# Mixer output weights moved into the value region of the ring, multiplied on four column groups and summed by an fp32 matmul

## The chip, the cores and the metric

The kernel runs on one core of one Trainium2 chip. The metric is the device time of one execution in microseconds (us). The time before is the median of nine runs; the profile is that of one execution. Engines: PE (matmul), DVE (vector), ACT (scalar), POOL (general), SP (here it only issues DMAs).

## What is computed

One decode step of a gated mix of two branches, all tensors in bf16, one token, width 1024:

```python
g = sigmoid((x * gate_w).sum(-1))
# branch a: 32 query heads, 4 key/value heads, 65536 cached positions, head size 128
q = x @ wq                                   # wq 1024 x 4096
a = softmax(q k^T / sqrt(128)) v  @ wo       # k, v: 4 x 65536 x 128 each; wo 4096 x 1024
# branch b: gated MLP over one position
z = gelu(x @ w_in)                           # w_in 1024 x 3584
z1, z2 = halves of z;  z2 = layernorm(z2)
b = (z1 * (w_sp * z2 + b_sp)) @ w_out        # w_out 1792 x 1024
out = g * a + (1 - g) * b
```

The two caches are 64 MiB each. All that is loaded comes to 162 MB.

## The kernel before

**Ordering.** Every instruction is recorded with the keys that it reads and writes (`Recorder.op`), and `plan` turns these into semaphore waits. Each engine runs its own instructions in the order in which they were recorded. A load waits until the last readers and writers of its slots are done, and SP issues the loads strictly in the order of the list `stream`: a load that waits holds up all behind it.

**The ring.** All large loads go into one ring of five areas of 4 MiB (32 KB on each partition). The first three are taken in turn by `kring()`; the last two together are the value region `VB`, which holds 8 MiB. `issue()` (L360) puts a load into SP's program as soon as the kernel's text has marked the earlier contents of its slots as used (`done`). The order of the loads is: the query weights (VB, two DMAs), K pages 0 and 1, the mixer's input weights `w_in` (VB, two DMAs), K pages 2 and 3, the mixer's output weights `w_out` (next ring slot, 3.5 MiB), and then six times a K page, a value load of two pages (VB, two DMAs) and a K page; at the end the last values and `wo`. A K page has 4 MiB; there are 16, four for each key/value head. L373 is the line of all these loads, on SP's queue.

**Start.** Small tables are built from an identity matrix (L389 to L406). x and the gate weights are loaded by ACT's queue (L279, called at L286 and L287) as two rows of 512. x is turned into columns by a product with two rows of the identity (L409) and eight matmuls (L414). The gate takes a product, a sum and a small matmul (L424 to L431). Then come the query matmuls on four column groups of PE (recorded at L442), and the query tables.

**K steps.** `k_step(n)` handles a K page in four pieces: DVE transposes a piece (L483, two buffers `ktb`), PE multiplies it with the padded queries (L493; all matmuls of the helper `mm` show L253 or L255). `score_piece` (L500) moves the scores to SBUF and takes their maximum. For pages that begin a head, `q_piece` (L471) first writes that head's queries. `exp_piece` (L516, ACT), `pt_piece` (L521, DVE) and `pv_piece` (L531, PE, into `obt`) handle the values of earlier pages inside later steps.

**Mixer.** `mixer_piece` (after K page 1) multiplies x with `w_in` into `obt`, and DVE and ACT do gelu and the normalisation (L595 to L625) up to `yb`, the 1792 inputs of the last product as 14 columns. `wout_piece` (after K page 3) multiplies them with `w_out` in 14 x 2 matmuls (L635), all into one partition of `obt`, and four ACT copies (L641) spread this row over partitions 0, 32, 64 and 96 of `brow`.

**End.** The `wo` matmuls (L706) run on four column groups and add up in `fbt`; DVE adds `brow` (L712), and SP writes the result (L715).

The order of the steps in the program, before:

```python
k_step(1, evac=0, own=True)
mixer_piece()
k_step(2)
k_step(3, evac=2)
wout_piece()
```

Of the kernel before, what the change touches and what calls it, by code (L numbers as in the profile page):

```python
# [8 lines left out]
ACTF = mybir.ActivationFunctionType  # L9
ALU = mybir.AluOpType  # L10
AXX = mybir.AxisListType.X
# [127 lines left out]
def bass_gated_mix__gqa_block_cached__mixer_gmlp__decode_kernel(  # L139
# [23 lines left out]
    FC = FH // 128  # L163
    OC = HQ * Dh // 128
# [10 lines left out]
    QW = DO // 4  # L175
# [15 lines left out]
    for name, n in [  # L191
        ("RING", NSUB * SUB), ("KT", NKT * 4096), ("SC", NSC * 2048), ("PSB", 1024), ("PTSB", 2 * 1024),
        ("QPAD", 4 * QP), ("IDB", 128), ("BM", 256), ("SEL", 16 * 32),
        ("M16", 32), ("MQ", 32), ("XT", KC), ("WB", 2), ("WBB", 4), ("ONEB", 128),
        ("MAXC", 2 * total), ("LP", 2 * total), ("COLS", 2 * 64), ("DM", 32), ("QALL", 128), ("OV", OC), ("MHALF", 4),
        ("YB", FC), ("BROW", 2 * QW), ("OROW", QW),
    ]:
        region(name, n)
    NA = (cur + 63) // 64 * 64
# [2 lines left out]
    def ab(name, n, o=0):  # L202
        return arena[:, OFF[name] + o:OFF[name] + o + n]

    def af(name, n, o=0):
        return arena[:, OFF[name] + 2 * o:OFF[name] + 2 * (o + n)].bitcast(F32)

    def vw(base, off, dims, p0=0, np_=128):
        ps = base.ap[0][0]
        return bass.AP(tensor=base.tensor, offset=base.offset + off + p0 * ps,  # L210
                       ap=[[ps, np_]] + [list(d) for d in dims])

    idb, bm, ones = ab("IDB", 128), af("BM", 128), af("SC", 128, 4 * 1024 + 896)
    sel, m16, mq = ab("SEL", 512), af("M16", 16), af("MQ", 16)
    xT, wb, wbb, oneb = ab("XT", KC), ab("WB", 2), af("WBB", 2), ab("ONEB", 128)
    qpad, qall = ab("QPAD", 4 * QP), ab("QALL", 128)
    maxc, lp, colt = af("MAXC", total), af("LP", total), af("COLS", 64)
    mhalf = af("MHALF", 2)
    yb, ovec, orow, brow = ab("YB", FC), ab("OV", OC), ab("OROW", QW), af("BROW", QW)
    dm = af("DM", 16)  # L220
    psb = ab("PSB", 1024)
    osc, ot = ab("PSB", 512), af("PSB", 128, 256)
    col = lambda i: colt[:, i:i + 1]
    (C_GS, C_GE, C_G1, C_G, C_OMG, C_MU, C_V, C_S0, C_R0, C_S1, C_R1, C_AL, C_BE, C_T) = range(14)
    C_G4 = 16

    def gcol(g, i):
        return col(C_G4 + 12 * g + i)

# [3 lines left out]
    scs = lambda n: af("SC", 1024, (n % NSC) * 1024)  # L233
# [7 lines left out]
    ob, mb, fb = obt[:, :], mbt[:, :], fbt[:, :]  # L241
    tb = scp[1][:, 0:512]
# [5 lines left out]
    P = R.op  # L248

    def mm(e, loaded, *a, **kw):  # L250

        if not loaded:
            return e.matmul(*a, **kw)  # L253
        with nc.discard():
            one = e.matmul(*a, **kw).ins  # L255
        return e.add_instruction(dataclasses.replace(one, name=nc.get_next_instruction_name(), ldweights=False))
# [4 lines left out]
    m32 = af("SC", 32, 4 * 1024 + 136)  # L261
# [5 lines left out]
    P("POOL", lambda e: e.memset(qpad, 0.0), w=["qpad"])  # L267
    P("DVE", lambda e: e.memset(ones, 1.0), w=["ones"])
    P("DVE", lambda e: e.memset(oneb, 1.0), w=["oneb"])
    P("DVE", lambda e: e.memset(brow, 0.0), w=["brow"])  # L270
    P("DVE", lambda e: e.memset(mb, 0.0), w=["mb"])
    P("DVE", lambda e: e.memset(ob, 0.0), w=["ob"])
    P("DVE", lambda e: e.memset(fb, 0.0), w=["fb"])
# [2 lines left out]
    def small(dst, src, key):  # L276
        def f(e):
            with nc.allow_non_contiguous_dma(reason="a few bytes"):
                return e.dma_start(dst, src)  # L279
        P("ACT", f, w=[key], dma="l%s" % (key if isinstance(key, str) else key[1]))  # L280


    xrow, grow, prod = ab("SC", 512, 3 * 2048), ab("SC", 512, 2 * 2048), af("SC", 512, 1 * 1024)
    xm = ab("SC", 1024, 3 * 2048 + 512)
    KX, KG, KP = ("sc", 3), ("sc", 2), ("sc", 1)
    small(xrow[0:2, :], A_x[0, 0].rearrange("(i n) -> i n", i=2), KX)  # L286
    small(grow[0:2, :], gate_w.rearrange("(i n) -> i n", i=2), KG)  # L287
    small(wb[0:1, 0:1], B_w_sp, "wsp")
    small(wb[0:1, 1:2], B_b_sp.rearrange("(a n) -> a n", a=1), "bsp")

# [7 lines left out]
    def load(keys, src, off):  # L298

        n = len(stream)  # L300
        w = src.shape[1]
        for i, key in enumerate(keys):
            place[key] = (n, off + i * (w // len(keys)), w // len(keys))
        stream.append((keys, off, src))

    def rows(w, i, c):

        return w[128 * c * i:128 * c * (i + 1), :].rearrange("(p c) n -> p (c n)", c=c)
# [10 lines left out]
    VB = KR * SUB  # L319
    ring = [0]  # L320

    def kring():
        s = ring[0] % KR
        ring[0] += 1
        return s * SUB

    def load_k(n):
        load([("k", n)], kv(A_k_cache, n), kring())
# [7 lines left out]
    load([("win", 0)], rows(B_w_in, 0, 8), VB)  # L336
    load_k(2)
    load_k(3)
    load([("wout", 0)], rows(B_w_out, 0, 14), kring())
    for i in range(6):  # L340
        load_k(2 * i + 4)
        load_v2(2 * i)
# [39 lines left out]
    def done(key):  # L382
# [8 lines left out]
    P("DVE", lambda e: e.tensor_copy(vw(bm, 0, [[8, 16], [1, 8]]), vw(m8, 0, [[0, 16], [1, 8]])), r=["m8"], w=["bm"])  # L391

    P("DVE", lambda e: e.tensor_reduce(m32, vw(idf, 0, [[1, 32], [32, 4]]), AXX, ALU.add), r=["idf"], w=["m32"])
    P("DVE", lambda e: e.tensor_copy(vw(sel, 0, [[16, 32], [1, 16]]), vw(m32, 0, [[1, 32], [0, 16]])),
      r=["m32"], w=["sel"])
    P("DVE", lambda e: e.tensor_reduce(mq, vw(idf, 0, [[1, 16], [16, 8]]), AXX, ALU.add), r=["idf"], w=["mq"])
    P("DVE", lambda e: e.tensor_reduce(mhalf, vw(idf, 0, [[32, 2], [64, 2], [1, 32]]), mybir.AxisListType.XY, ALU.add),
      r=["idf"], w=["mhalf"])
# [4 lines left out]
    for fe in range(4):  # L403
        P("DVE", lambda e, fe=fe: e.tensor_copy(vw(sele, 128 * fe, [[32, 4], [1, 32]]),
                                                vw(idb, 64 * (fe // 2) + fe % 2, [[0, 4], [2, 32]])),
          r=["idb"], w=[KSE])  # L406


    P("DVE", lambda e: e.tensor_tensor(vw(xm, 0, [[512, 2], [1, 512]], 0, 2), vw(xrow, 0, [[0, 2], [1, 512]], 0, 2),  # L409
                                       vw(idb, 0, [[1, 2], [0, 512]], 0, 2), ALU.mult), r=[KX, "idb"], w=["xm"])  # L410

    def f(e):
        for c in range(KC):
            ins = e.matmul(tb[:, c:c + 1], vw(xm, c, [[512, 2], [8, 64]], 0, 2), oneb[0:2, 0:1], start=(c == 0),  # L414
                           stop=(c == KC - 1), skip_group_check=True)
        return ins
    P("PE", f, r=["xm", "oneb"], w=[KTB])
# [2 lines left out]
      r=["oneb", "wsp", "bsp"], w=["mb"])  # L420
    P("DVE", lambda e: e.tensor_copy(wbb, mb[:, 0:2]), w=["wbb", "mb"])


    P("DVE", lambda e: e.tensor_tensor(prod[0:2, :], xrow[0:2, :], grow[0:2, :], ALU.mult), r=[KX, KG], w=[KP])  # L424
    P("DVE", lambda e: e.tensor_reduce(col(C_GS)[0:2, :], prod[0:2, :], AXX, ALU.add), r=[KP], w=["gs"])
    P("PE", lambda e: e.matmul(tb[:, 0:1], ones[0:2, :], col(C_GS)[0:2, :], start=True, stop=True),
      r=["ones", "gs"], w=[KTB])
    P("ACT", lambda e: e.activation(col(C_GE), tb[:, 0:1], ACTF.Exp, scale=-1.0), w=["ge", KTB])
    P("DVE", lambda e: e.tensor_scalar(col(C_G1), col(C_GE), 1.0, None, op0=ALU.add), r=["ge"], w=["g1"])
# [2 lines left out]
      r=["g"], w=["omg"])  # L432
# [195 lines left out]
    def wout_piece():  # L628
        sl, keys = use(("wout", 0))

        def f(e):
            for c in range(FC):
                for s in range(2):
                    o = DO * c + 512 * s
                    ins = mm(e, s > 0, ob[0:1, 512 * s:512 * (s + 1)], yb[:, c:c + 1], sl[:, o:o + 512],  # L635
                             start=(c == 0), stop=(c == FC - 1), tile_position=(0, 0), skip_group_check=True)
            return ins
        P("PE", f, r=["yb"] + keys, w=["ob"])
        done(("wout", 0))
        for q in range(4):  # L640
            P("ACT", lambda e, q=q: e.activation(brow[32 * q:32 * q + 1, :], ob[0:1, QW * q:QW * (q + 1)], ACTF.Copy),  # L641
              w=["brow", "ob"])


    def k_step(n, evac=None, gmax=None, pts=(), own=False, late=None):

        for p in range(4):
            k_piece(n, p)
            if p == 0 and evac is not None:
                score_piece(evac)  # L650
                if gmax is not None:
                    max_first(gmax)
            if p == 1 and gmax is not None:
                max_second(gmax)
            if p == 1 and pts:
                exp_piece(pts[0])
            if p == 2 and pts:
                pt_piece(pts[0])
                exp_piece(pts[1])
            if p == 3 and pts:  # L660
                pt_piece(pts[1])
            if late is not None:
                (out_second, out_third, out_fourth, lambda g: None)[p](late)
        if own:
            score_piece(n)
# [2 lines left out]
    k_step(1, evac=0, own=True)  # L668
    mixer_piece()
    k_step(2)  # L670
    k_step(3, evac=2)
    wout_piece()
    for i in range(6):
        a = 2 * i + 4
        k_step(a, evac=a - 1, gmax=(a - 1) // NP if a % NP == 0 else None, pts=(2 * i, 2 * i + 1), own=True)
# [23 lines left out]
    for i, c0, c1 in [(0, 0, 8), (1, 0, 8), (2, 0, 8), (3, 0, 4), (3, 4, 6), (3, 6, 8)]:  # L699
        sl, keys = use(("wo", i, c0))  # L700

        def f(e, i=i, sl=sl, c0=c0, c1=c1):
            for c in range(c0, c1):
                for q in range(4):
                    o = DO * (c - c0) + QW * q
                    ins = e.matmul(fb[32 * q:32 * q + 1, 0:QW], ovec[:, 8 * i + c:8 * i + c + 1],  # L706
                                   sl[:, o:o + QW], start=(i == 0 and c == 0), stop=(i == 3 and c == 7),
                                   tile_position=(0, 32 * q), skip_group_check=True)
            return ins
        P("PE", f, r=[("ovec", i)] + keys, w=["fb"])  # L710
        done(("wo", i, c0))
    P("DVE", lambda e: e.tensor_tensor(orow[0:97, :], fb[0:97, 0:QW], brow[0:97, :], ALU.add),  # L712
      r=["brow"], w=["orow", "fb"])
    osrc = bass.AP(tensor=arena, offset=OFF["OROW"], ap=[[32 * NA, 4], [1, QW]])
    P("SP", lambda e: e.dma_start(out[0, 0].rearrange("(q n) -> q n", n=QW), osrc), r=["orow"], w=["out"], dma="out")  # L715

# [29 lines left out]
```

## Time and profile before

| what | value |
|---|---|
| median of nine runs | 386.42 us (385.35 to 387.38) |
| the profiled execution | 385.69 us |
| its span | 383.9 us |
| PE, DVE, ACT busy | 234.9, 212.3, 25.8 us |
| read from HBM | 162.01 MB, 422 GB/s over the span |
| mean granted PE clock | 0.865 |

The span is the time between the first and last event of the profiled execution. "Chain that ended last" follows the work back from the last instruction to whatever released it. A DMA's "to landing" counts from its issue by the engine, so it holds the time for which it stood in the queue. In a timeline line the columns are start, duration (us), engine, line, operation, output and input, count, and in brackets the idle time before with what ended it. A window's line gives its bounds and length, the busy time of PE, PE's weight loads, DVE, ACT and POOL, and then the granted clock, the DMA share and GB/s.

### The profile page before, as it was taken

The numbers are of one execution on the slowest core, as the hardware profiler recorded it, in microseconds if no ns is written. First come the engines' busy times: TensorE is split into PE (matmuls) and PEld (weight loads), VectorE is DVE, ScalarE is ACT, GpSimd is POOL, SyncE is SP. The second block draws the span as 40 slices with busy tenths as digits, with TensorE's granted clock in tenths as the row PEclk, the third lists the DMA queues.
The fourth block names the chain that finished last, engine by engine and source line by source line (L and its number), as shares of the span: only waits on it lengthen the run. The fifth ranks groups of instructions, "written<-read, shape, count | busy, mean of one in ns | idle before, by whom it ended". The sixth has DMA issues, their size and how long they took to land.

```text
span 383.9 us, 2520 instructions
## 1 busy us (share of the span) xinstructions
PE 234.9 (61%) x1367; PEld 57.8 (15%) x777; DVE 212.3 (55%) x229; ACT 25.8 (7%) x42; POOL 1.5 (0%) x8
## 2 busy tenths in 40 slices
PE   0064755197975478737794867365839671848363
PEld 0011111111211011201220112011201120112131
DVE  6107961779780598057944990479448913842020
ACT  1000000100240001000210010001200100031000
POOL 1000000000000000000000000000000000000000
PEclk9996996579999699879696998699978997869777
DMA  8999999999999999999999999999999999999995
GB/s 328 437 437 437 435 435 436 434 390 437 429 417 430 427 430 432 437 437 434 434 429 437 427 420 429 430 437 435 437 427 435 430 434 420 423 434 435 425 424 218
DMA packets 6222, 162.16 MB, mean 422 GB/s; under 512 B 700, under 2 KB 708, under 8 KB 964
## 3 DMA queue, kind: packets, MB, share of 16 engines
q1 hardware_dynamic: 6200, 162.01, 98.5%
q8 instruction: 8, 0.13, 0.1%
q14 instruction: 2, 0.02, 0.0%
q10 hardware_dynamic: 12, 0.00, 0.0%
HBM read 162.01 MB, written 0.00 MB: 422 GB/s over the span
## 4 chain that ended last, share of the span: by engine, by line
DMA 63%; DVE 18%; PE 16%; SPq 1%; issue 1%; ACT 0%
DMA arena<-in_A_k_cache_dram 33%; DVE arena L483 12%; DMA arena<-in_A_v_cache_dram 8%; DMA arena<-in_B_w_in_dram 8%; DMA arena<-in_A_wo_dram 8%; DMA arena<-in_A_wq_dram 6%; PE obt L253 5%; PE obt L255 5%; PE scp L253 3%; PE scp L255 2%; SPq L373 1%; DVE arena L500 1%; DVE arena L521 1%; DVE arena L556 1%; DVE arena L554 1%
## 5 line engine op out<-in xcount | busy, mean ns | idle before, releaser
L483 DVE STREAM_TRANSPOSE arena<-arena 128x2048 f32<-128x2048 f32 x64 | 145.2, 2293 | 81.9 <-DMA arena<-in_A_k_cache_dram 73.8
L253 PE MATMUL scp<-arena 128*128 128x512 bf16 x256 | 108.5, 424 | 85.7 <-DVE arena L483 62.2
L255 PE MATMUL scp<-arena 128*128 128x512 bf16 x256 | 107.3, 419 | 0.0
L253 PE MATMUL obt<-arena 128*64 128x512 bf16 (+2 forms) x334 | 69.9, 442 | 31.7 <-DMA arena<-in_A_v_cache_dram 14.0
L255 PE MATMUL obt<-arena 128*64 128x512 bf16 (+2 forms) x334 | 69.4, 438 | 0.0
L253 PEld LDWEIGHTS scp<-arena 128*128 128x128 bf16 x256 | 26.9, 105 | 190.5 <-DVE arena L483 96.0
L253 PEld LDWEIGHTS obt<-arena 128*64 128x64 bf16 (+1 forms) x334 | 20.8, 118 | 92.5 <-issue 87.9
L516 ACT ACTIVATE arena<-arena 128x1024 bf16<-128x1024 f32 x16 | 18.4, 1150 | 223.2 <-DVE arena L512 112.5
L500 DVE TENSOR_SCALAR_CACHE_REDUCE arena<-scp 128x1024 f32<-128x1024 f32 x16 | 19.3, 1205 | 9.3 <-PE scp L255 9.3
L521 DVE STREAM_TRANSPOSE arena<-arena 128x1024 bf16<-128x1024 bf16 x16 | 19.4, 1213 | 8.1 <-PE obt L255 5.5
L706 PE MATMUL fbt<-arena 128*1 128x256 bf16 x128 | 6.7, 371 | 4.3 <-DMA arena<-in_A_wo_dram 4.2
L546 DVE RECIPROCAL arena<-mbt 128x1 f32<-128x1 f32 x4 | 0.6, 139 | 15.8 <-PE mbt L542 15.8
L448 DVE CAST arena<-obt 97x1024 bf16<-97x1024 f32 x1 | 1.2, 1225 | 13.0 <-PE obt L255 13.0
L595 DVE COPY arena<-obt 128x896 f32<-128x896 f32 x1 | 1.1, 1093 | 10.2 <-PE obt L255 10.2
L471 DVE COPY arena<-arena 32x32 bf16<-32x32 bf16 x16 | 2.7, 166 | 6.2 <-PE scp L255 6.0
L712 DVE TENSOR_TENSOR arena<-fbt,arena 97x256 bf16<-97x256 f32 x1 | 0.4, 425 | 10.2 <-PE fbt L706 10.2
L414 PE MATMUL scp<-arena 2*128 2x1 bf16 x8 | 0.6, 198 | 7.0 <-DVE arena L409 7.0
L706 PEld LDWEIGHTS fbt<-arena 128*1 128x1 bf16 x128 | 3.4, 107 | 7.5 <-DMA arena<-in_A_wo_dram 4.7
L602 ACT ACTIVATE arena<-arena 128x28 f32<-128x28 f32 x1 | 0.2, 227 | 53.8 <-DVE arena L601 53.8
L641 ACT ACTIVATE arena<-obt 1x256 f32<-1x256 f32 x4 | 1.5, 373 | 30.6 <-PE obt L255 30.6
L419 PE MATMUL mbt<-arena 1*128 1x2 bf16 x1 | 0.2, 158 | 5.2 <-DMA arena<-in_B_b_sp_dram 5.2
L608 PE MATMUL mbt<-arena 128*128 128x1 f32 x2 | 0.6, 362 | 4.3 <-DVE arena L607 4.3
(86 smaller groups left out, 51.7 us busy)
## 6 DMA issues: line engine op xcount, KB each, us to landing
arena<-in_A_k_cache_dram SPq DMA_DIRECT2D x16, 4096.0 KB, 38.1
arena<-in_A_v_cache_dram SPq DMA_DIRECT2D x16, 4096.0 KB, 31.6
arena<-in_A_wq_dram SPq DMA_DIRECT2D x2, 4096.0 KB, 16.7
arena<-in_A_wo_dram SPq DMA_DIRECT2D x3, 2048.0 KB, 23.8
arena<-in_B_w_in_dram SPq DMA_DIRECT2D x1, 4096.0 KB, 24.1
arena<-in_B_w_out_dram SPq DMA_DIRECT2D x1, 3584.0 KB, 35.5
arena<-in_B_w_in_dram SPq DMA_DIRECT2D x1, 3072.0 KB, 31.1
arena<-in_A_wo_dram SPq DMA_DIRECT2D x1, 1024.0 KB, 27.7
```

Source lines behind the costliest of these rows:

```text
L253: return e.matmul(*a, **kw)
L255: one = e.matmul(*a, **kw).ins
L373: P("SP", lambda e, o=OFF["RING"] + off + c, m=m, src=src[:, c:c + m]: e.dma_start(arena[:, o:o + m], src), w=[("slot", x) for x in grains ...
L471: P("DVE", lambda e, pb=pb: e.tensor_copy(vw(qpad, 24 + 32 * pb, [[QP, 4], [1, 8]], 32 * pb, 32), vw(qall, 8 * g, [[32, 4], [1, 8]], 32 * ...
L483: P("DVE", lambda e: e.transpose(ktb(i).bitcast(F32), sl[:, 4096 * p:4096 * (p + 1)].bitcast(F32)), r=keys[2 * p:2 * p + 2], w=[("kt", i % ...
L500: P("DVE", lambda e: e.tensor_scalar(scs(n), sc_ps(n), 0.0, None, op0=ALU.add, op1=ALU.max, accum_out=maxc[:, n:n + 1]), w=[("sc", n % NSC ...
L516: P("ACT", lambda e: e.activation(psb, scs(n), ACTF.Exp, bias=gcol(n // NP, K_NB), scale=SCALE, accum_out=lp[:, n:n + 1]), r=[("sc", n % N ...
L521: P("DVE", lambda e: e.transpose(ptsb(n), psb), r=["psb"], w=[("ptsb", n % 2)])
L554: P("DVE", lambda e: e.tensor_scalar(osc, ob[:, 0:512], gcol(g, K_FA), None, op0=ALU.mult), r=[("fh", g, 0)], w=["psb", "ob"])
L556: P("DVE", lambda e: e.scalar_tensor_tensor(osc, ob[:, 512:1024], gcol(g, K_FB), osc, op0=ALU.mult, op1=ALU.add), r=[("fh", g, 1), "psb"], ...
L641: P("ACT", lambda e, q=q: e.activation(brow[32 * q:32 * q + 1, :], ob[0:1, QW * q:QW * (q + 1)], ACTF.Copy), w=["brow", "ob"])
L706: ins = e.matmul(fb[32 * q:32 * q + 1, 0:QW], ovec[:, 8 * i + c:8 * i + c + 1], sl[:, o:o + QW], start=(i == 0 and c == 0), stop=(i == 3 a ...
```

## The change

1. `w_out` is loaded into the value region `VB` and no longer into a ring slot, so all later K pages (and the last ring loads) move by one slot. The stream's order stays.
2. `wout_piece` moves ahead of `k_step(3)`. Its matmuls go to four column groups in turn (chunk c to group c % 4), into partitions 0, 32, 64 and 96 of `obt`.
3. One ACT copy moves these partial rows to `part`, a score buffer, and four fp32 matmuls with a column of ones at those partitions (`C_E4`, a new copy at the start) sum them into `fbt`, where the `wo` matmuls later add up. `brow` and its memset go, and the last DVE instruction is a copy.
4. x and the gate weights are loaded and used as 8 rows of 128.

```diff
-    small(xrow[0:2, :], A_x[0, 0].rearrange("(i n) -> i n", i=2), KX)
-    small(grow[0:2, :], gate_w.rearrange("(i n) -> i n", i=2), KG)
+    small(xrow[0:8, 0:128], A_x[0, 0].rearrange("(i n) -> i n", i=8), KX)
+    small(grow[0:8, 0:128], gate_w.rearrange("(i n) -> i n", i=8), KG)
...
-    load([("wout", 0)], rows(B_w_out, 0, 14), kring())
+    load([("wout", 0)], rows(B_w_out, 0, 14), VB)
...
+    P("DVE", lambda e: e.tensor_copy(col(C_E4), m32[:, 0:1]), r=["m32"], w=["e4"])
...
-    P("DVE", lambda e: e.tensor_tensor(vw(xm, 0, [[512, 2], [1, 512]], 0, 2), vw(xrow, 0, [[0, 2], [1, 512]], 0, 2),
-                                       vw(idb, 0, [[1, 2], [0, 512]], 0, 2), ALU.mult), r=[KX, "idb"], w=["xm"])
+    P("DVE", lambda e: e.tensor_tensor(vw(xm, 0, [[128, 8], [1, 128]], 0, 8), vw(xrow, 0, [[0, 8], [1, 128]], 0, 8),
+                                       vw(idb, 0, [[1, 8], [0, 128]], 0, 8), ALU.mult), r=[KX, "idb"], w=["xm"])
...
-            ins = e.matmul(tb[:, c:c + 1], vw(xm, c, [[512, 2], [8, 64]], 0, 2), oneb[0:2, 0:1], start=(c == 0),
+            ins = e.matmul(tb[:, c:c + 1], vw(xm, c, [[8, 128]], 0, 8), oneb[0:8, 0:1], start=(c == 0),
...
-    P("DVE", lambda e: e.tensor_tensor(prod[0:2, :], xrow[0:2, :], grow[0:2, :], ALU.mult), r=[KX, KG], w=[KP])
+    P("DVE", lambda e: e.tensor_tensor(prod[0:8, 0:128], xrow[0:8, 0:128], grow[0:8, 0:128], ALU.mult), r=[KX, KG], w=[KP])
...
             for c in range(FC):
+                j = c % 4
                 for s in range(2):
                     o = DO * c + 512 * s
-                    ins = mm(e, s > 0, ob[0:1, 512 * s:512 * (s + 1)], yb[:, c:c + 1], sl[:, o:o + 512],
-                             start=(c == 0), stop=(c == FC - 1), tile_position=(0, 0), skip_group_check=True)
+                    ins = mm(e, s > 0, ob[32 * j:32 * j + 1, 512 * s:512 * (s + 1)], yb[:, c:c + 1], sl[:, o:o + 512],
+                             start=(c < 4), stop=(c >= FC - 4), tile_position=(0, 32 * j), skip_group_check=True)
             return ins
         P("PE", f, r=["yb"] + keys, w=["ob"])
         done(("wout", 0))
-        for q in range(4):
-            P("ACT", lambda e, q=q: e.activation(brow[32 * q:32 * q + 1, :], ob[0:1, QW * q:QW * (q + 1)], ACTF.Copy),
-              w=["brow", "ob"])
+        part = scs(4)
+        P("ACT", lambda e: e.activation(part[0:97, :], ob[0:97, :], ACTF.Copy), w=[("sc", 4), "ob"])
+
+        def f(e):
+            for q in range(4):
+                ins = e.matmul(fb[32 * q:32 * q + 1, 0:QW], col(C_E4)[0:97, :], part[0:97, QW * q:QW * (q + 1)],
+                               start=True, stop=False, tile_position=(0, 32 * q), skip_group_check=True)
+            return ins
+        P("PE", f, r=["e4", ("sc", 4)], w=["fb"])
...
     k_step(2)
+    wout_piece()
     k_step(3, evac=2)
-    wout_piece()
...
-                                   sl[:, o:o + QW], start=(i == 0 and c == 0), stop=(i == 3 and c == 7),
+                                   sl[:, o:o + QW], start=False, stop=(i == 3 and c == 7),
...
-    P("DVE", lambda e: e.tensor_tensor(orow[0:97, :], fb[0:97, 0:QW], brow[0:97, :], ALU.add),
-      r=["brow"], w=["orow", "fb"])
+    P("DVE", lambda e: e.tensor_copy(orow[0:97, :], fb[0:97, 0:QW]), w=["orow", "fb"])
```

More of the change, by code (lines that the diff above doesn't have):

```diff
@@ L195, in bass_gated_mix__gqa_block_cached__mixer_gmlp__decode_kernel @@
         ("MAXC", 2 * total), ("LP", 2 * total), ("COLS", 2 * 64), ("DM", 32), ("QALL", 128), ("OV", OC), ("MHALF", 4),
-        ("YB", FC), ("BROW", 2 * QW), ("OROW", QW),
+        ("YB", FC), ("OROW", QW),
     ]:
@@ L218, in bass_gated_mix__gqa_block_cached__mixer_gmlp__decode_kernel @@
     mhalf = af("MHALF", 2)
-    yb, ovec, orow, brow = ab("YB", FC), ab("OV", OC), ab("OROW", QW), af("BROW", QW)
+    yb, ovec, orow = ab("YB", FC), ab("OV", OC), ab("OROW", QW)
     dm = af("DM", 16)
@@ L224, in bass_gated_mix__gqa_block_cached__mixer_gmlp__decode_kernel @@
     (C_GS, C_GE, C_G1, C_G, C_OMG, C_MU, C_V, C_S0, C_R0, C_S1, C_R1, C_AL, C_BE, C_T) = range(14)
-    C_G4 = 16
+    C_E4, C_G4 = 14, 16
     def gcol(g, i):
@@ L269, in bass_gated_mix__gqa_block_cached__mixer_gmlp__decode_kernel @@
     P("DVE", lambda e: e.memset(oneb, 1.0), w=["oneb"])
-    P("DVE", lambda e: e.memset(brow, 0.0), w=["brow"])
     P("DVE", lambda e: e.memset(mb, 0.0), w=["mb"])
@@ L421, in bass_gated_mix__gqa_block_cached__mixer_gmlp__decode_kernel @@
     P("DVE", lambda e: e.tensor_copy(wbb, mb[:, 0:2]), w=["wbb", "mb"])
-    P("DVE", lambda e: e.tensor_tensor(prod[0:2, :], xrow[0:2, :], grow[0:2, :], ALU.mult), r=[KX, KG], w=[KP])
-    P("DVE", lambda e: e.tensor_reduce(col(C_GS)[0:2, :], prod[0:2, :], AXX, ALU.add), r=[KP], w=["gs"])
-    P("PE", lambda e: e.matmul(tb[:, 0:1], ones[0:2, :], col(C_GS)[0:2, :], start=True, stop=True),
+    P("DVE", lambda e: e.tensor_tensor(prod[0:8, 0:128], xrow[0:8, 0:128], grow[0:8, 0:128], ALU.mult), r=[KX, KG], w=[KP])
+    P("DVE", lambda e: e.tensor_reduce(col(C_GS)[0:8, :], prod[0:8, 0:128], AXX, ALU.add), r=[KP], w=["gs"])
+    P("PE", lambda e: e.matmul(tb[:, 0:1], ones[0:8, :], col(C_GS)[0:8, :], start=True, stop=True),
       r=["ones", "gs"], w=[KTB])
```

## The prediction, made before the changed kernel was run

> **What bounds the kernel now.** I read the page's slices and queues first, then the chain that ended last, the SP engine's timeline, the DMA issues in short windows, and the PE and DVE timelines around the output weights.
>
> Page: DMA share by slice, bytes by slice, the queue, shares of the chain.
> ```profile
> DMA  8999999999999999999999999999999999999995
> GB/s 328 437 437 437 435 435 436 434 390 437 429 417 430 427 430 432 437 437 434 434 429 437 427 420 429 430 437 435 437 427 435 430 434 420 423 434 435 425 424 218
> q1 hardware_dynamic: 6200, 162.01, 98.5%
> DMA 63%; DVE 18%; PE 16%; SPq 1%; issue 1%; ACT 0%
> ```
> The load stream is full from the first slice to the last: 162.01 MB at about 437 GB/s are 371 us of a 383.9 us span. PE (61%) and DVE (55%) have room. So only three things move the end: the start (slice 1), the tail after the last load (slice 40), and holes in the stream. One early slice stands out: the ninth (76.8 to 86.4 us, 390 GB/s). Beside it stand two-microsecond windows (last two columns: DMA share, GB/s):
> ```profile
> 84.00:86.00 2.00, 1.33 (x7) 0.29 (x3) 2.00 (x2) 0.00 (x0) 0.00 (x0) 1.00 0.93 401
> 86.00:88.00 2.00, 1.72 (x9) 0.30 (x4) 2.00 (x2) 0.00 (x0) 0.00 (x0) 1.00 0.95 291
> ```
> The chain and SP's timeline (start, duration) tell why:
> ```profile
> 83.19 2.33 DVE arena L483
> 85.54 0.33 SPq L373
> ```
> ```profile
> 29.73 13.43 SPq L373 DMA_DIRECT2D arena<-in_A_k_cache_dram  x2
> 52.76 0.33 SPq L373 DMA_DIRECT2D arena<-in_B_w_out_dram  x1
> 85.54 0.33 SPq L373 DMA_DIRECT2D arena<-in_A_k_cache_dram  x1
> 85.91 0.91 SPq L373 DMA_DIRECT2D arena<-in_A_v_cache_dram  x2
> 95.46 8.43 SPq L373 DMA_DIRECT2D arena<-in_A_k_cache_dram  x2
> 117.02 5.51 SPq L373 DMA_DIRECT2D arena<-in_A_v_cache_dram  x2
> ```
> K page 4 goes into the ring slot of page 2, so its load waits for page 2's last transpose (85.5 us). That one is late because DVE spent 66.16 to 74.4 us on the mixer. Times from issue to landing, by windows around the issues of page 3, output weights and page 4:
> ```profile
> arena<-in_A_k_cache_dram SPq DMA_DIRECT2D x1, 4096.0 KB, 36.9
> arena<-in_B_w_out_dram SPq DMA_DIRECT2D x1, 3584.0 KB, 35.5
> arena<-in_A_k_cache_dram SPq DMA_DIRECT2D x1, 4096.0 KB, 12.7
> ```
> Page 3 landed at 42.8 + 36.9 = 79.7 us, the output weights at 88.3, page 4 at 98.2. The first half of the first value load (85.91 us, 22.8 us to landing) came at 108.7 and the second (86.38 + 32.01) at 118.4. A 4096 KB load in the full stream takes 9.7 us (the two query-weight loads land 0.74 + 12.1 = 12.8 and 1.19 + 21.32 = 22.5 us). So 79.7 to 118.4 should have been 8.5 + 3 x 9.7 = 37.6 us and was 38.7: 1.1 us lost, because from 79.7 us the output weights were the only load in the queue, until page 4's was issued 2.8 us ahead of their end.
>
> **Part 1, output weights into the value region.** All later K pages move one ring slot on. Page 4 takes page 1's slot, free since 52.7 us (SP issued the output weights then, on that release). The output weights now need the input weights consumed: their last matmul ends near 66.1 us. So both are issued at about 66.1 and 66.5 us instead of 52.8 and 85.5. Their turns do not move: page 3 is in transfer until 79.7 us, so the output weights still land at 88.3, and page 4 follows without a hole. Gain: from the landings 1.1 us; from the bytes between 76 and 128 us (windows in sequence, 22.03 MB against 52 us x 430 GB/s, the mean of the long window 157 to 376 us) 0.8 us. I take 0.9. The lowest end is 0.2: page 4's last landing alone came 9.9 us after the output weights', against 9.7, and only the last of the 16 DMA engines sets the end.
>
> What is late next is the first value load, which now waits for the output matmuls. Behind it on SP stand its second half and pages 5 and 6. It must be issued before page 4 is nearly through. Without the hole page 4 ends at 98.2 - 0.9 = 97.3 us. The first load of all was issued at 0.74 us and slice 1 lost a quarter, 328 of 437 GB/s, of 9.6 us, or 2.4 us, that is 1.7 us of lead. Page 4 had 2.8 us of lead and still left a hole; the engines do not end together. I take 2.8: deadline 94.5 us.
>
> The Trainium skill ("DMA: Bandwidth & Descriptors", the table of two cost components) gives each DMA a fixed part of about 2.0 us beside bytes at 436 GB/s. Queued loads here show none of it (9.7 us for 4.19 MB). If the starved load paid all of it, the gain would be 2.0 us; the landings show 1.1.
>
> **Part 2, four column groups, earlier.** The output matmuls move ahead of page 3 on PE. The first line is the old form, the second the query weights, which already go to four groups:
> ```profile
> 97.33 0.38 PE L253 MATMUL obt<-arena 128*1 128x512 bf16 x1
> ...
> 22.64 0.60 PE L253 MATMUL obt<-arena 128*1 128x512 bf16 x4 [7.52 <-DMA arena<-in_A_wq_dram]
> ...
> 87.75 0.33 PEld L253 LDWEIGHTS scp<-arena 128*128 128x128 bf16 x2 [0.99 <-DVE arena L483]
> ...
> 128.13 4.51 DVE L483 STREAM_TRANSPOSE arena<-arena 128x2048 f32<-128x2048 f32 x2 [13.45 <-DMA arena<-in_A_k_cache_dram]
> ```
> Old: 28 matmuls 0.215 us apart, 6.0 us. New: four in 0.215 us at full clock (0.43 at the half clock of 22.64), so 28/4 x 0.215 = 1.5 us, at most 3.0. PE has page 2 done at about 87.3 us (page 3 starts at 87.75), waits for the landing at 88.3, and is through at 89.8 to 91.3. The value load is then issued about 90.5 us, 4 us ahead of the deadline. Cost on the stream: none.
>
> **Part 3, the sum by fp32 matmul.** ACT copies 97x1024 once: 1.15 us by its own row of 128x1024 (L516), against 4 x 0.373 now. Then four fp32 matmuls of 256 columns. No row shows one this wide. The fp32 matmuls of one column leave two records each (L608), so the lower end is two passes as narrow as L706 (128 in 6.7 us: 8 are 0.4 us) and the upper 8 x 0.43 = 3.4 us; I take 1.0, near L706, which also uses four groups and 256 columns. PE waits for ACT, and page 3's matmuls, page 4's and the first PV stand behind it. Page 3 then begins on PE at 90.5 + 1.2 + 1.0 = 92.7 instead of 87.8 and ends near 102 instead of 97.3; the old output matmuls ended at 103.4, so PE reaches page 4 no later. DVE, whose copies of the next queries wait for page 3, starts page 4 some 5 us later. Cover: DVE stood idle 13.45 us before 128.13 for page 5's load. Page 6's load needs page 3's last transpose, about 100 us, and its turn comes after 128 us. The next value load was issued at 117.0 and landed 30.5 us later; its own transfer is 9.7 of these, so about 20 us of delay would fit. Without that cover, 5 us would be the price; with it, 0.
>
> **Part 4, x and gate in 8 rows; small things.** Two issues on ACT's queue, as before. DVE starts the x product at 5.76 us with no DMA wait, has it in column form at 7.88, and PE uses it at 22.64: 14.8 us of cover. The gate needs its chain (ending 15.9 us) before 28.89 us on DVE and before 22.6 on PE (its matmul ends at 15.1): 7.5 us. The two gate operations shrink from 512 to 128 columns (0.67 us each to some 0.25), off the path; one 0.27 us memset goes, one copy of about 0.17 comes. The final addition (0.42 us on the path) becomes a copy of 256 columns; between the casts of 128 columns (0.29) and 1024 (1.225) that is 0.42. Cost 0, at most 0.05 either way.
>
> Against the 8 rows speaks the Trainium skill's quick figures ("DMA: Bandwidth & Descriptors"): below 512 B a transfer falls to read-modify-write, and these rows have 256 B. No run here shows such a load. Even at 2.0 us apiece in a row, by that page's fixed part, 8 would be 16 us, and this would delay the first matmul by an estimated 1 to 2 us.
>
> **Sum.** The profiled execution took 385.69 us (span 383.9, 1.8 around it), 0.7 under the median of nine. The gain of 0.9 would make it 384.8; carried to the median, 386.42 - 0.9 = **385.5 us**. One measurement of this kernel can tell about 0.2% (0.77 us) from no change.
>
> **Rivals.**
> 1. The hole goes, the end barely moves. The 16 engines each carry their own share, the slowest ends the stream, and it may have idled least (0.2 us, above). For it: page 4's step of 9.9. Against: the value load behind it took 10.5 us, so the loss did reach the last engine by then. Time 386.2, no measurable change. It covers also a partly lost gain.
> 2. Slower: the value region becomes the bottleneck. One mechanism: the first value load is issued after page 4 is drained. It decides at 94.5 us, 6.2 us after the output weights land. If the groups ran one after another at the half clock, 28 x 0.43 = 12.0 us, the issue would come at 100.3, 5.8 us late; less the 0.9 saved, 4.9 us are lost: 391.3. For it: PE had the half clock at 76.7 to 82.4 us. Against: the query weights do overlap in the same order of groups, the clock is full from 84 us on (1.00 in the windows), and even serial at full clock ends at 94.3.
> 3. The rows of x and gate land late. It decides when x comes after 22.6 us; then each microsecond delays the input weights' issue, which itself has a lead of about 13 us (28.88 against their turn at 42). Before that point, 385.5. It is part of the unseen below.
>
> **Chances.** The forecast 0.62, rival 1 0.24, rival 2 0.09, something unseen in the start or tail 0.05. Of the forecast, with 0.8 to 1.1 us against a bound of 0.77 and runs 2 us apart, about 0.53 lies beyond the bound and 0.09 within. So faster 0.53, same 0.33, slower 0.14 (rival 2 and the unseen). Range: low end 386.42 - 1.1 and 0.4 for the spread of a median, 384.9; high end past rival 1 by the same spread and a little of the unseen, 386.8.
>
> **What would show it.** In the profile after: output weights and page 4 issued together near 66 us; the ninth and tenth slices at about 435 GB/s; the first value load issued at 90 to 91.5 us and landing 9.7 us after page 4; output matmuls in groups of four at about 88.5 us; DVE still idle before page 5; the last load landing 0.9 us earlier. A stretch of low GB/s at 97 to 105 us, or page 4 and the value load more than 10 us apart, would make it wrong.

## The result, and the profile after

| | before | after |
|---|---|---|
| median | 386.64 us (43 runs, 385.27 to 387.60) | 385.30 us (14 runs, 385.13 to 385.53) |
| profiled execution (span) | 385.69 us (383.9) | 385.37 us (383.6) |

The ratio is 0.9966, 95% interval 0.9957 to 0.9976: the changed kernel is 1.3 us faster, and its runs lie within 0.4 us where those of before spread over 2.3 us. The two profiled executions differ by only 0.32 us, since that of before was one of its fastest. This difference between profile and median turned out to be half of the story. The experiments below ran in three further sets, each beside runs of the kernel before, whose medians there were 386.15, 386.20 and 386.88 us; the kernels with a full stream had 385.23 to 385.33 everywhere. The gain is thus 0.9 to 1.6 us, by the runs of before with which it is compared.

SP's timeline of the kernel after, around the moved load (start, duration):
```profile
65.78 0.33 SPq L372 DMA_DIRECT2D arena<-in_B_w_out_dram  x1
66.15 0.43 SPq L372 DMA_DIRECT2D arena<-in_A_k_cache_dram  x1
90.29 0.80 SPq L372 DMA_DIRECT2D arena<-in_A_v_cache_dram  x2
91.13 7.59 SPq L372 DMA_DIRECT2D arena<-in_A_k_cache_dram  x2
118.56 3.78 SPq L372 DMA_DIRECT2D arena<-in_A_v_cache_dram  x2
```
Page 4 is issued at 66.15 us, right behind the output weights, where before it came at 85.54. The first value load is issued at 90.29 us, when the output matmuls are through. The windows in which the stream had its hole (last two columns: DMA share, GB/s):
```profile
84.00:86.00 2.00, 1.32 (x7) 0.29 (x3) 2.00 (x2) 0.00 (x0) 0.00 (x0) 1.00 1.06 459
86.00:88.00 2.00, 0.90 (x5) 0.10 (x1) 2.00 (x2) 0.00 (x0) 0.00 (x0) 1.00 1.21 520
```
The 291 GB/s of 86 to 88 us are now 520. The window behind it is lower again, and was 508 before:
```profile
88.00:90.00 2.00, 1.65 (x28) 0.38 (x14) 2.00 (x3) 0.00 (x0) 0.00 (x0) 1.00 0.87 377
```
A single window of 2 us therefore proves little. Over 84 to 90 us the mean is 452 GB/s, against 400 before. PE, ACT and DVE around the moved step, from the timeline:
```profile
88.35 0.39 PE L253 MATMUL obt<-arena 128*1 128x512 bf16 x4 [1.45 <-DMA arena<-in_B_w_out_dram]
...
90.29 1.02 ACT L642 ACTIVATE arena<-obt 97x1024 f32<-97x1024 f32 x1 [17.71 <-PE obt L255]
...
91.37 0.61 PE L646 MATMUL fbt<-arena 97*1 97x256 f32 x8 [1.12 <-ACT arena L642]
...
101.09 2.31 DVE L483 STREAM_TRANSPOSE arena<-arena 128x2048 f32<-128x2048 f32 x1
...
127.19 4.50 DVE L483 STREAM_TRANSPOSE arena<-arena 128x2048 f32<-128x2048 f32 x2 [10.97 <-DMA arena<-in_A_k_cache_dram]
```
Four matmuls now run together, and the last pair begins at 89.86 us. The fp32 sum has eight records (two for each matmul) and takes 0.61 us. DVE begins page 4 at 101.09 instead of 98.23 us (before: the line below) and still waits 10.97 us for page 5 afterwards: the delay has vanished there.
```profile
98.23 2.31 DVE L483 STREAM_TRANSPOSE arena<-arena 128x2048 f32<-128x2048 f32 x1
```

**A measure for the hole.** The trace records the landings of the 16 shares of a load, one for each DMA engine. Below, for every profiled kernel, is the time from the landing of K page 3 to that of value page 1 as a mean over the engines (four loads; 37.74 us where the stream is full), then the mean and the last landing of the very last load, and the number of packets of 24 KB or more between 84 and 104 us that took over 1.35 us (the median packet takes 1.21). "Behind" is how far the last engine lands after the mean. Apart from before and after, the names are the runs of the experiments below, in this order: ring_only, sum_only, rows_only, no_rows, mixer_late, two_groups, late_wout, before_slow, after_slow, before_again_1 and 2, more_fetch.

```
kernel           profiled us   page 3 -> value 1   last load: mean   last    behind   long packets
before              385.69         38.56              380.07        380.90    0.83        16
before_again_1      387.37         38.96              380.40        382.39    1.99        28
before_again_2      387.14         38.52              379.97        382.15    2.17        24
rows_only           387.08         38.70              380.15        382.10    1.96        19
sum_only            387.13         38.52              379.99        382.15    2.16        18
before_slow         386.72         39.22              380.71        381.75    1.04        17
ring_only           386.75         38.34              379.79        381.77    1.99        21
late_wout           389.69         42.12              383.62        384.73    1.11        15
mixer_late          385.29         37.74              379.21        380.27    1.06         0
two_groups          385.27         37.74              379.21        380.29    1.08         1
no_rows             385.17         37.74              379.18        380.19    1.01         1
after_slow          385.53         37.74              379.19        380.54    1.35         1
after               385.37         37.74              379.33        380.38    1.06         1
more_fetch          388.61         38.64              380.44        383.66    3.22        15
```

The rows are of two kinds: full stream, at most one long packet, 385.2 to 385.5 us; or a hole, 15 and more long packets, and more time. From the last landing to the end of the span it is 3.0 to 3.2 us in every row.

### The profile page after: what moved, and what is told of

Its sections match the earlier page's. It is cut to its first block, busy times and chain, and to the rows that moved or that the text cites. A ratio compares the mean times of both kernels' runs of the same rounds, so it can differ in the third digit from the quotient of the medians.

```text
span 383.6 us, 2533 instructions
## 1 busy us (share of the span) xinstructions
PE 230.0 (60%) x1375; PEld 56.1 (15%) x785; DVE 211.3 (55%) x229; ACT 25.3 (7%) x39; POOL 1.5 (0%) x8
## 4 chain that ended last, share of the span: by engine, by line
DMA 61%; DVE 18%; PE 18%; SPq 1%; issue 1%; ACT 1%
DMA arena<-in_A_k_cache_dram 33%; DVE arena L483 13%; DMA arena<-in_B_w_in_dram 8%; DMA arena<-in_A_wo_dram 8%; DMA arena<-in_B_w_out_dram 6%; PE obt L253 6%; DMA arena<-in_A_wq_dram 6%; PE obt L255 5%; PE scp L253 3%; PE scp L255 3%; DVE arena L500 1%; DVE arena L521 1%; SPq L372 1%; DVE arena L471 1%; DVE arena L556 0%
## 5 line engine op out<-in xcount | busy, mean ns | idle before, releaser
L253 PE MATMUL obt<-arena 128*64 128x512 bf16 (+2 forms) x334 | 65.1, 435 | 32.2 <-DMA arena<-in_A_v_cache_dram 12.6
L255 PE MATMUL obt<-arena 128*64 128x512 bf16 (+2 forms) x334 | 64.5, 430 | 0.0
L253 PEld LDWEIGHTS obt<-arena 128*64 128x64 bf16 (+1 forms) x334 | 19.5, 116 | 88.7 <-issue 79.9
L556 DVE SCALAR_TENSOR_TENSOR arena<-obt,arena 128x512 bf16<-128x512 f32 x4 | 3.0, 751 | 0.1
```

Of the source, the lines that this page charges most:

```text
L556: P("DVE", lambda e: e.scalar_tensor_tensor(osc, ob[:, 512:1024], gcol(g, K_FB), osc, op0=ALU.mult, op1=ALU.add), r=[("fh", g, 1), "psb"], ...
```

## The experiments

Theory: the hole after the output weights is the cost, and the change removes it because page 4's load no longer waits for page 2. Rivals: the shorter PE work, the 8 rows, or the place in the ring by itself.

### The parts one at a time

**The ring move and the order alone** (28 serial matmuls, four ACT copies and `brow` as before):
```diff
-    load([("wout", 0)], rows(B_w_out, 0, 14), kring())
+    load([("wout", 0)], rows(B_w_out, 0, 14), VB)
...
     k_step(2)
+    wout_piece()
     k_step(3, evac=2)
-    wout_piece()
```


> Only the ring move and the earlier place of the output matmuls; they stay serial on one partition, with the four ACT copies and brow. Theory (the hole in the load stream was the whole cost): page 4 is issued at 66 us and the ninth slice is full; 28 serial matmuls at full clock end at 88.3 + 6.0 = 94.4 us, so the first value load is issued right at the deadline of 94.5 us and a hole of 0 to 0.4 us may be left: 1.0 to 1.3 us under the kernel before (385.3 to 385.7), with runs as close together as after's (within 0.4 us). Rival (the column groups or the rows of x bring the gain): no change, runs 2 us apart as before.

Measured: 386.78 us median (12 runs, 385.25 to 387.61), ratio 1.001, 0.9996 to 1.0024: no gain, which taken by itself is what the rival expected. But the hole had moved. Its SP timeline:
```profile
66.01 0.43 SPq L373 DMA_DIRECT2D arena<-in_A_k_cache_dram  x1
94.57 0.80 SPq L373 DMA_DIRECT2D arena<-in_A_v_cache_dram  x2
```
and its windows:
```profile
94.00:96.00 2.00, 2.00 (x10) 0.38 (x4) 0.00 (x0) 1.39 (x4) 0.00 (x0) 1.00 1.01 393
96.00:98.00 2.00, 2.00 (x10) 0.38 (x4) 1.57 (x1) 1.39 (x2) 0.00 (x0) 1.00 0.87 344
```
Page 4 is early, but the value load at 94.57 us, as computed for serial matmuls, is already too late: 408 GB/s over 92 to 100 us (449 in the run with two column groups below, which lost nothing although it too has a low window, 360 GB/s, from 96 to 98 us), a mean loss of 38.34 - 37.74 = 0.60 us, and the last engine 1.99 us behind the mean instead of 1.06. Moving the load alone trades one hole for another; that the hole and not the missing groups is to blame is shown by the runs of the mixer and of two groups below.

**The groups and the fp32 sum alone** (output weights in the ring slot, matmuls after page 3):
```diff
-        load([("wout", 0)], rows(B_w_out, 0, 14), VB)       # against the changed kernel
+        load([("wout", 0)], rows(B_w_out, 0, 14), kring())
...
-    wout_piece()
     k_step(3, evac=2)
+    wout_piece()
```
(x and gate in 2 rows, too.)

> Only the four column groups with the fp32 sum; output weights stay in the ring slot, their matmuls after page 3, x and gate in 2 rows. Theory: they lie off the stream, so the same time as before within 0.2% (386.6), page 4 still issued at about 85.5 us, runs still 2 us apart. Rival (the shorter PE work brings the gain): 0.5 to 1.3 us faster.

Measured: 386.96 us (12 runs, 385.81 to 387.56), ratio 1.0017, 1.0004 to 1.003: within 0.2%, no gain, if anything a little slower than the 386.15 of before beside it. Page 4 is issued at 84.06 us and the hole is there (mean loss 0.78 us):
```profile
84.06 0.33 SPq L372 DMA_DIRECT2D arena<-in_A_k_cache_dram  x1
```
The rival of shorter PE work falls.

**The 8 rows alone** (the hunks on `xrow`, `grow`, `xm` and `prod` of the change):

> Only x and gate in 8 rows. Theory: the same time as before within 0.2% (386.6), runs still 2 us apart. Rival (the small loads on two of the DMA engines are what made the runs of before spread and their median high): median 0.5 to 1.0 us lower and the runs within 0.5 us.

Measured: 386.61 us (12 runs, 385.48 to 387.45), ratio 1.0003, 0.9988 to 1.0017. No change.

**Everything but the 8 rows:**

> The whole change without the 8 rows: x and gate in 2 rows as before. Theory: the same as the changed kernel, 385.3 us within 0.2, runs within 0.5 us of each other. Rival (the rows matter): some of the gain is missing, 385.7 to 386.6, or the runs lie 2 us apart.

Measured: 385.23 us (12 runs, 385.17 to 385.44), ratio 0.9978, 0.9969 to 0.9986 (the runs of before on this chip had a median of 386.15). The rows bring nothing; ring move, order and groups together bring all.

### The hole closed through another door

```diff
     k_step(1, evac=0, own=True)
-    mixer_piece()
     k_step(2)
+    mixer_piece()
     k_step(3, evac=2)
     wout_piece()
```


> The kernel before with one edit: the mixer step after K step 2 instead of before it, so that page 2 is used up, and page 4 issued, without waiting for the mixer's DVE work. Nothing of the change under study is in it. Theory (the hole is the cause): page 4 is issued near 79 to 80 us, some 7 us before its turn, the value load near 86 us as before; no hole, so 385.3 us like the changed kernel, runs within 0.5 us of each other. Rival (earlier output matmuls, groups or the ring place bring the gain by themselves): 386.2 to 386.6 as before, runs 2 us apart.

Measured: 385.33 us (12 runs, 385.16 to 385.53), ratio 0.9977, 0.9963 to 0.999. SP's timeline and a window of this kernel:
```profile
80.90 0.33 SPq L373 DMA_DIRECT2D arena<-in_A_k_cache_dram  x1
86.03 0.80 SPq L373 DMA_DIRECT2D arena<-in_A_v_cache_dram  x2
...
86.00:88.00 2.00, 0.00 (x0) 0.00 (x0) 1.93 (x2) 0.00 (x0) 0.00 (x0) 1.00 1.17 504
```
This is the kernel before with two lines exchanged. It issues page 4 at 80.90 us, some 6 us before the mean landing of the output weights (86.85), and has the whole gain, the narrow spread included. It has no ring move, no groups, no fp32 sum: the hole is the cause.

### Where the deadline lies

**Two column groups instead of four:**
```diff
-                j = c % 4
+                j = c % 2
...
-                             start=(c < 4), stop=(c >= FC - 4), tile_position=(0, 32 * j), skip_group_check=True)
+                             start=(c < 2), stop=(c >= FC - 2), tile_position=(0, 32 * j), skip_group_check=True)
```
(the copy and the sum take 33 partitions instead of 97)

> The changed kernel with two column groups instead of four: the output matmuls take 14 x 0.215 = 3.0 us instead of 1.5, and the first value load is issued at about 91.8 us instead of 90.3. Theory: the groups matter only through this issue, and 91.8 still lies before the deadline (somewhere between 91 and 94.5): 385.3 us, runs within 0.5 us. Rival (the deadline lies earlier, or fewer groups cost by themselves): 385.6 to 386.8 with runs 1 to 2 us apart.

Measured: 385.26 us (12 runs, 385.12 to 385.45), ratio 0.9976, 0.9964 to 0.9988. The value load is issued here:
```profile
91.60 0.80 SPq L372 DMA_DIRECT2D arena<-in_A_v_cache_dram  x2
```
No hole. The groups count through this issue alone; two are enough.

**The output matmuls after page 3** in the otherwise changed kernel (the order of `k_step(3)` and `wout_piece()` as before):

> The changed kernel, but the output matmuls stay after page 3. Theory: they end at about 98.8 us, so the first value load is issued some 4.3 us after the predicted deadline of 94.5 (5 to 6 us after one of 93 to 93.5, as the run of the ring move alone, issued at 94.57 with a mean loss of 0.5 us, suggests). The hole costs 4.3 to 6 us over the changed kernel: 389.6 to 391.3. Rival (the value load's issue does not matter while page 4 is under way or later loads make it up): under 387.0.

Measured: 389.26 us (6 runs, 388.83 to 389.69), ratio 1.0076, 1.0054 to 1.0098, a little under the expected range. Its SP timeline and windows:
```profile
98.99 0.80 SPq L372 DMA_DIRECT2D arena<-in_A_v_cache_dram  x2
...
96.00:98.00 2.00, 2.00 (x26) 0.39 (x13) 0.67 (x4) 0.00 (x0) 0.00 (x0) 1.00 0.07 25
98.00:100.00 2.00, 0.95 (x16) 0.09 (x2) 1.83 (x1) 1.00 (x1) 0.00 (x0) 1.00 0.30 82
```
The stream stands still, and nothing later makes it up. The mean loss is 42.12 - 37.74 = 4.38 us. The value load was issued 2.4 us after the mean landing of page 4 (96.57 us); the other 2.0 us are an estimate, by this difference, of what it costs to start in an empty queue. The first packets begin at 99.95 us, 1.0 us after the issue, and 15 of the first 16 take 1.48 to 2.06 us instead of 1.21. If the loss grew one to one with a late issue, it would count from 98.99 - 4.38 = 94.6 us on; this is one run, so that slope is not shown. Yet 94.57 in the run of the ring move cost 0.60 in the mean and the whole gain in the median, and 91.6 cost nothing. A queue that drains on some engines before others costs earlier than one counts back from a full drain.

### Page 4 later on purpose

```diff
     mixer_piece()
+    for i in range(2):
+        P("DVE", lambda e, i=i: e.transpose(ptsb(i)[0:96, :], psb[0:96, :]), r=["psb"], w=[("ptsb", i)])
```


> The kernel before with two idle DVE transposes of 96 partitions x 1024 (about 1.2 us each) between the mixer and page 2. Theory (page 4's issue waits for DVE's work, one to one): page 4 issued at about 88 us instead of 85.5, the hole 2.4 us wider, median 388.5 to 389.1. Rival (the hole is not fed by this wait): 386.2 to 386.8.

Measured: 386.79 us (10 runs, 385.94 to 388.54), ratio 1.0014, 0.9996 to 1.0033: the expected size was wrong, and by the time alone the run lies in the rival's range. What speaks for the theory is in its one profile. The added work shows in DVE's timeline, and the issue on SP's:
```profile
73.76 2.36 DVE L671 STREAM_TRANSPOSE arena<-arena 96x1024 bf16<-96x1024 bf16 x2
76.05 4.46 DVE L483 STREAM_TRANSPOSE arena<-arena 128x2048 f32<-128x2048 f32 x2
81.72 6.70 DVE L483 STREAM_TRANSPOSE arena<-arena 128x2048 f32<-128x2048 f32 x3 [1.21 <-PE scp L255]
...
86.25 0.33 SPq L373 DMA_DIRECT2D arena<-in_A_k_cache_dram  x1
```
Page 4 came at 86.25 us, 0.7 to 2.2 us later than in the other kernels with page 4 behind page 2 (84.06 to 85.54), not 2.4 later. The mean loss grew to 39.22 - 37.74 = 1.48 us from 0.78 to 1.22. But in the profiled execution the engines came out of this hole closer together (1.04 us behind the mean at the end, against 2.0 to 2.2 in most), which would explain why the median hardly rose; the other executions were not profiled.

**The same addition to the changed kernel:**

> The changed kernel with the same two idle DVE transposes between mixer and page 2. In the kernel before they moved page 4's issue by some 1.3 us and the mean landing by 0.7. Theory (page 4 no longer waits for DVE's work): page 4 still issued near 66 us, the first value load by 92 us at the latest, no hole: 385.3 us within 0.2, runs within 0.5 us. Rival (DVE's chain still feeds the stream): 385.9 to 386.7.

Measured: 385.30 us (8 runs, 385.19 to 385.54), ratio 0.9964, 0.9952 to 0.9976. Page 4 and the value load are issued here:
```profile
66.88 0.43 SPq L372 DMA_DIRECT2D arena<-in_A_k_cache_dram  x1
91.26 0.80 SPq L372 DMA_DIRECT2D arena<-in_A_v_cache_dram  x2
```
The stream is full; this delay of DVE no longer reaches it.

### What spreads the runs

**Two more profiles of the kernel before**, one execution each:

> The kernel before, unchanged, for a further profile of it. Theory (a hole of 0.6 to 1.0 us in every execution, and a spread of 2 us from which DMA engines are late when the hole has passed and are then hit again by a fetch): again a mean step of 10.4 to 10.7 us from the output weights' landing to page 4's, whatever the total; the total between 385.3 and 387.6 goes with how far the last engine is behind the mean. Rival (the spread is that of the hole's width): the step differs by as much as the totals.

> The kernel before once more, with the same expectations: theory, a mean step of 10.4 to 10.7 us from the output weights' landing to page 4's and a total that goes with how far the last engine is behind the mean; rival, a step that differs as much as the totals.

Measured: 387.37 and 387.14 us, against 385.69 of the first profile. The steps from the output weights to page 4 are 11.03 and 10.60 us against 10.54, so the first lies outside the expected range. By the table, the mean last landing differs by +0.33 and -0.10 us and the distance of the last engine behind it by +1.16 and +1.34; the totals differ by 1.68 and 1.45. So in these three profiles the scatter among the engines carries most of the difference, not the width of the hole.

**More instruction fetches** in the changed kernel:
```diff
                 run("POOL", e)
+                for _ in range(2048):
+                    e.wait_ge(sems["POOL"], 1)
```


> The changed kernel with 2048 more waits, all already met, at the end of POOL's program, where nothing depends on them; they are there to be fetched. Theory (each fetch of instructions takes its turn on one of the 16 DMA engines and makes that engine late by 0.7 to 1.4 us, and an engine that is hit twice is late twice): 8 to 16 more packets in the queues for instructions, the mean last landing 0.5 to 1.0 us later, the last one 0.7 to 1.5 us later: 386.0 to 386.8. Rival (fetches cost the loads nothing): 385.3.

Measured: 388.65 us (6 runs, 388.46 to 389.12), ratio 1.0051, 1.0034 to 1.0068. Its queues:
```profile
q8 instruction: 8, 0.13, 0.1%
q14 instruction: 10, 0.08, 0.1%
```
Queue q14 had 2 such packets in the kernel after. The sign is as expected and the size far above it. From load to load the last share falls further behind the mean, 1.9 us at K page 1 and 4.8 us at the output weights (0.5 and 1.3 in the kernel after), while the last but one is 1.1 us behind there. The packets do not name their engine, so that one engine took nearly all of the added fetches is read from this. The output matmuls had to wait for the late share, the value load was issued at 95.55 us instead of 90.29 (line below), and a hole was back (38.64). So more fetches do delay a load's last share, and a late share can bring a hole.
```profile
95.55 1.84 SPq L374 DMA_DIRECT2D arena<-in_A_v_cache_dram  x2
```

## Why the prediction was right, point by point

**The hole and its cause: right.** Page 4's wait for page 2 was the cost. Predicted issues near 66.1 and 66.5 us, measured 65.78 and 66.15; predicted value load about 90.5, measured 90.29; the value load landed 9.71 us after page 4.

**The sum: the mechanism right, one term mis-sized.** The hole was taken at 0.9 us, for the profiled execution and for the median alike. The mean loss is 0.82, 1.22 and 0.78 us in the three profiles of before, 0.94 on average. But the end is set by the last engine, and the prediction carried the one profile to the median as if the other runs differed by something unrelated. In that profile the last engine was 0.83 us behind the mean; in the two others 1.99 and 2.17, and 1.06 in the kernel after. So the profile pair gains only 0.52 at the last landing (380.90 to 380.38), while the other two gain 2.01 and 1.77. The median gained 1.3 here and 0.9 to 1.6 in the other sets of runs. Nor is the gain the same for every execution: 13 of the 122 runs of before took no longer than the slowest of after (385.53 us), and the fastest of both lie at 385.1. None of these was profiled; the change takes away the slower runs and not a fixed amount from each. That 385.5 us lies so near the measured 385.30 is in part luck: the nine runs from which it starts had a median 0.2 us under that of the 43, and the gain was 0.4 us larger.

**Rival 1: in part true of the profiled execution, but not of most others.** It held that the last engine may have idled least, so that the gain would be lost among the engines. In the first profile of before, part of it was (0.82 us in the mean, 0.52 at the last landing). In five of the eight profiles with a hole and no added fetches the hole does the opposite: it leaves the last engine 2.0 to 2.2 us behind the mean (1.0 to 1.35 without a hole).

**Part 2, the deadline: right where all engines are drained, too late otherwise.** 94.5 us was predicted; the full drain gives 94.6 if the loss counts one to one. The step that failed is the lead of 2.8 us on which 94.5 rests: before's page 4 had this lead over the last landing ahead of it and left a hole, so it could not mark the safe side. The run of the ring move had 3.5 us of such lead and lost, the run of two groups 6.5 and lost nothing. Accordingly the sentence under rival 2, that even serial matmuls at full clock would cost nothing, failed: at 94.57 us the gain was gone. The true edge lies between 91.6 and 94.57. The forecast did not need it, as 90.29 is clear of both; the faster matmuls, costed as work with 4 us to spare, were necessary, although two column groups suffice.

**Rival 2: its mechanism exists.** With the matmuls after page 3 it costs 4.0 us over the changed kernel's median.

**Part 3 and the cover: right.** ACT's copy 1.02 us (1.2 predicted), the sum 0.61 (1.0), page 3 on PE from 91.91 (92.7). DVE was 2.9 us late at page 4 instead of 5, and idled 10.97 us before page 5.

**Part 4: right.** No effect of the 8 rows. The Trainium skill's warning of small rows ("DMA: Bandwidth & Descriptors", Specifications) has no cost to show here: with 256 B rows the product of x starts at 5.75 us in the run of the rows alone, against 5.76. The last copy takes 0.425 us, as the addition did.

**The fixed part of 2.0 us** (same page, "Anatomy of one DMA — SWDGE (gpsimd) path", the table of two cost components; it is given there for DMAs that GpSimd issues, and these loads are issued by SP): a load issued while the queue ran dry lost 0.6 to 1.5 us in the mean in these runs, a queued one nothing. The one load that met an empty queue lost an estimated 2.0 us beyond the lateness of its issue, which agrees with the figure.

**Two signs failed.** The last load was to land 0.9 us earlier; in the pair of profiles it was 0.52. The ninth and tenth slices were to show about 435 GB/s; they show 424 and 425, as do slices with a full stream:
```profile
GB/s 332 434 437 437 436 415 447 420 424 425 434 437 437 437 436 434 424 437 420 420 432 437 437 437 436 424 427 435 413 434 436 437 434 437 437 419 424 425 424 198
```
In slices or windows this short a few large packets decide; the landings show the hole better.

**Open:** what exactly scatters the engines. In the two further profiles of before, the last engine is 2.8 and 3.0 us behind the mean already when page 4 lands, while a fetch fell at 98.7 and 98.4 us. In the run of the groups alone it is 1.3 behind there and 2.2 at the end, so something later was added. That fetches take part is shown by the run with more of them; how they and the long packets share the scatter is not separated.

## What to carry to other kernels

Where the load stream is the bound, look for each load's wait and for its lead over the moment at which the queue ahead of it runs dry. Here 5 us ahead of the mean landing of the load before were safe, 0.6 to 2.8 us were not, and about 2 us cost the whole gain although the mean over the engines showed a loss of only 0.60. A slot freed earlier helps only if whatever takes over that slot's old role is early as well: here the ring move needed the faster matmuls, and an exchange of two steps did the same with neither. If the runs of a kernel spread far more than those of its neighbour, take several profiles before reading a sum off one.

## What the runs showed of the hardware

Around a hole the packets are slow: 15 to 28 packets took over 1.35 us, up to 2.65, against 1.21 in the full stream, where there was none or one. In the first profile of before these 16 packets together took 0.59 us per engine more than at 1.21 each, beside a mean loss of 0.82; so not all that a hole costs is idle time. At the end the last of the 16 DMA engines is up to 2.2 us behind the mean (1.0 to 1.35 without a hole). Later loads even this out only in part: in the second and third profile of before it was 2.8 and 3.0 us when page 4 landed and 2.0 and 2.2 at the end. Fetches of instructions show in the trace as DMA packets: one of 16 KB took about 1.0 us, one of the 8 KB packets added on q14 about 0.31. Eight more of these made the changed kernel 3.3 us slower.
